# Lower parts of the first MLP's weights: subtracted on VectorE or on GpSimd

## The chip, the cores and the metric

The kernel runs on one core of a Trainium2 chip. The metric is the device time of one execution in microseconds (us). The engines are named as the profile names them: PE (TensorE matmul), PEld (its weight load), DVE (VectorE), ACT (ScalarE), POOL (GpSimd) and SP (the queue that issues all the DMAs here).

## The reference

An attention with pooled keys and values, then two MLPs, over 8 batches of 576 tokens (4608 rows of 512):

```
k_p, v_p = mean of k and v over each 8 neighbouring positions        # 72 keys per head
attn     = softmax(q k_p^T / sqrt(64)) v_p                           # 8 heads of 64
x        = attn as 4608 x 512
x        = (sigmoid(x @ w_gate) * (x @ w_val)) @ w_out               # d_ff 1536
out      = elu(x @ w_in2) @ w_out2                                   # d_ff 2048
```

`q`, `k`, `v` are float32. The five weight matrices are float64, and the kernel reads each as pairs of 32-bit integers.

## The kernel before

The matmuls take float32 operands in two parts, an upper one (`hi`, the value as `fp32r`) and a lower one (`lo`, the value less `hi`), and make three passes over them (`PASSES`). The 4608 tokens go in 12 blocks (`n`) of 384. In a block the first MLP loops over 12 columns of d_ff (`c`), 128 wide each: `emit_gate` for the gate (L493), `emit_sig` (L501), `emit_gate` for the value, `emit_g` (the product, L505, split into `hi` and `lo`), and for the column before, `emit_y` (L512). `emit_pv`, `emit_s`, `emit_t` and their like do the attention of the next block between these. The second MLP follows in six strips.

The weights of the first MLP must be narrowed from float64 to float32 and split before they are used. There are 36 jobs, three for each column (gate, value, out), and each is one 128x512 tile `nt`:

- `fetch_to`: a DMA brings the raw 64-bit words into a tile `rw` of the ring `raw` (4 buffers).
- `open_to`: ACT takes the magnitude of the high words into `nt` (L180; 3 buffers).
- `narrow_1`: two DVE instructions on `nt` (L102, L106).
- `narrow_2`: two DVE instructions that put in the sign and the low bits (L112, L116).
- `halves`, which calls `split`: ACT writes the upper part into `wg` or `wo` (L89), and POOL subtracts it from `nt` for the lower part (L90).

`convert` does one step of this pipe: it opens the job after the next, interleaves on DVE L112 of job i-1, L102 of job i, L116 of job i-1, L106 of job i, and then splits job i-1. Five calls of `convert` stand ahead of the first block, and block 0 calls it three times in each column. Below, A is the call between the two `emit_gate`, B the one behind the second, C the one behind `emit_g`. The jobs end in column 10 with `settle`, so that four splits lie ahead of block 0 and 32 in it. The order on every engine is the order of the code (`manual_schedule`), and each engine works through its own instructions in that order.

Besides these, POOL has in block 0 the lower part of `g` (L90, one per column), the normalization of the attention's weights `p` (L431), the lower part of the pooled values `vhl` (L368) and the placed values `vbd` (L376). The other callers of `split` for `pt` and `x` name DVE, and `emit_g` and the second MLP's `elu` leave it with POOL. The second MLP's weights are prepared in later blocks, where `lower` (L233) makes the same subtraction of 128x512 on DVE.

Of the kernel before, what the change touches and what calls it, by code (L numbers as in the profile page):

```python
# [9 lines left out]
F32 = mybir.dt.float32  # L10
# [14 lines left out]
def fused_kernel(  # L25
# [23 lines left out]
    nc = tc.nc  # L49
# [32 lines left out]
    def f32(ap):  # L82
        return ap.bitcast(F32)
# [4 lines left out]
    def split(dst_hi, dst_lo, src, eng=nc.gpsimd):  # L88
        nc.scalar.activation(out=dst_hi, in_=src, func=AF.Copy)  # L89
        eng.tensor_tensor(out=dst_lo, in0=src, in1=f32(dst_hi), op=ALU.subtract)  # L90
# [50 lines left out]
    def halves(dst):  # L141
        def done(t):
            hi, lo = dst()
            split(hi, lo, t.bitcast(F32))
        return done

    jobs = []
# [864 lines left out]
```

## Time and profile before

| | us |
|---|---|
| median of 3 runs | 1951.27 (1950.71 to 1951.61) |
| the profiled execution, its own time | 1944.64 |
| its span in the profile | 1942.9 |
| PE busy | 1842.2 (95%) |
| DVE busy | 915.6 (47%) |
| ACT busy | 794.0 (41%) |
| POOL busy | 509.3 (26%) |

The profiled execution took 1.74 us more than its span, and stands 6.6 us under the median of the runs. Times in the views count from the span's start. The busy share of an engine is an average over the whole program; the page also has it in 40 slices of 48.6 us, and the views of a stretch give it for a part of the program. In the rows, `out<-in` are the names of tiles, `xN` is the count, and what stands in brackets or behind the last bar is the time for which the engine sat idle before the instruction, and what ended it.

### The profile page before, as it was taken

How to read it: one execution, taken by the hardware profiler on the slowest of the kernel's cores; microseconds unless marked ns; L12 is line 12 of the kernel's file. 1: busy time of each engine (PE TensorE's matmuls, PEld its weight loads, DVE VectorE, ACT ScalarE, POOL GpSimd, SP SyncE). 2: the span in 40 equal slices, each digit the busy share in tenths (PEclk: the TensorE clock that was granted, in tenths of full speed). 3: DMA queues.
4: the chain of work that ended last, by engine and by line, in shares of the span. 5: the costliest groups of instructions: out<-in, count | busy, mean ns of one | idle time of the engine just before them, and what ended most of it. 6: DMA issues, size and time to landing. Idle time of an engine off the chain costs nothing.

```text
span 1942.9 us, 25840 instructions
## 1 busy us (share of the span) xinstructions
PE 1842.2 (95%) x9996; PEld 1735.3 (89%) x9996; DVE 915.6 (47%) x1531; ACT 794.0 (41%) x1499; POOL 509.3 (26%) x523
## 2 busy tenths in 40 slices
PE   4777999999989999899999999999999999999999
PEld 3666989989989999899999998989999998999988
DVE  7997445554545554533422223443444344443432
ACT  3544334333334343333333224444454444444443
POOL 4455212222213232113121112222222222222222
PEclk7889999999999999999999999999999999999999
DMA  7332224232223332320201244334343353343430
GB/s 216 109 124 87 79 82 126 97 96 79 80 90 117 111 102 93 95 73 23 63 3 28 77 146 188 127 125 168 114 179 118 125 190 125 132 163 135 163 114 33
DMA packets 112603, 213.49 MB, mean 110 GB/s; under 512 B 43616, under 2 KB 66656, under 8 KB 112480
## 3 DMA queue, kind: packets, MB, share of 16 engines
q1 hardware_dynamic: 112480, 211.84, 32.1%
q8 instruction: 78, 1.28, 0.3%
q14 instruction: 45, 0.37, 0.1%
HBM read 169.87 MB, written 41.94 MB: 109 GB/s over the span
## 4 chain that ended last, share of the span: by engine, by line
PE 61%; DVE 2%; DMA 1%; ACT 1%; issue 1%; SPq 0%; POOL 0%; DVEq 0%; ACTq 0%; POOLq 0%
PE oacc L893 20%; PE bank L847 18%; PE gv L493 13%; PE acc L512 7%; PE xv L473 1%; DVE ks L346 1%; PE atv L473 1%; PE ats L406 1%; DMA rkv<-in_k_dram 0%; DMA rw<-in_moe_w_out_dram 0%; PE att L446 0%; PE atq L396 0%; ACT L501 0%; DMA rkv<-in_v_dram 0%; DVE pt L90 0%
## 5 line engine op out<-in xcount | busy, mean ns | idle before, releaser
L493 PE MATMUL gv<-x,wg 128*128 128x384 f32 x3456 | 658.3, 344 | 20.2 <-DVE sg L505 18.5
L493 PEld LDWEIGHTS gv<-x,wg 128*128 128x128 f32 x3456 | 613.6, 193 | 25.7 <-ACT wo L89 11.9
L893 PE MATMUL oacc<-w2o,gc 128*128 128x512 f32 x1728 | 452.4, 393 | 2.8 <-ACT yl L536 2.5
L893 PEld LDWEIGHTS oacc<-w2o,gc 128*128 128x128 f32 x1728 | 319.1, 187 | 51.4 <-ACT yl L536 2.8
L847 PE MATMUL bank<-form,wr 128*128 128x384 f32 x1728 | 353.1, 339 | 1.5 <-DVE ea L860 1.4
L90 POOL TENSOR_TENSOR g<-sg,g 128x384 fp32r<-128x384 f32 x144 | 155.0, 1076 | 748.3 <-ACT g L89 748.3
L847 PEld LDWEIGHTS bank<-form,wr 128*128 128x128 f32 x1728 | 314.4, 188 | 25.2 <-DVE ea L860 1.7
L512 PE MATMUL acc<-g,wo 128*128 128x384 f32 x1728 | 327.0, 336 | 1.7 <-POOL g L90 1.7
L512 PEld LDWEIGHTS acc<-g,wo 128*128 128x128 f32 x1728 | 302.1, 188 | 5.0 <-POOL g L90 2.9
L505 DVE TENSOR_TENSOR sg<-sg,gv 128x384 f32<-128x384 f32 x144 | 79.3, 550 | 341.6 <-PE gv L493 341.1
L90 POOL TENSOR_TENSOR gc<-ea,gc 128x384 fp32r<-128x384 f32 x96 | 98.1, 1022 | 300.2 <-ACT gc L89 297.1
L90 POOL TENSOR_TENSOR gc<-eb,gc 128x384 fp32r<-128x384 f32 x96 | 97.9, 1019 | 261.3 <-ACT gc L89 240.8
L501 ACT ACTIVATE sg<-gv 128x384 f32<-128x384 f32 x144 | 70.7, 491 | 233.2 <-PE gv L493 232.9
L89 ACT ACTIVATE g<-sg 128x384 fp32r<-128x384 f32 x144 | 75.5, 524 | 178.0 <-DVE sg L505 177.9
L856 ACT ACTIVATE eb<-u 128x384 f32<-128x384 f32 x96 | 50.4, 525 | 129.5 <-DVE u L877 129.3
L860 DVE SCALAR_TENSOR_TENSOR eb<-eb,u 128x384 f32<-128x384 f32 x96 | 53.6, 558 | 99.6 <-ACT eb L857 99.6
L856 ACT ACTIVATE ea<-bank 128x384 f32<-128x384 f32 x48 | 23.6, 492 | 157.8 <-PE bank L847 157.8
L90 DVE TENSOR_TENSOR pt<-att,pt 128x512 fp32r<-128x512 f32 x72 | 34.7, 486 | 111.2 <-ACT pt L89 111.0
L860 DVE SCALAR_TENSOR_TENSOR ea<-ea,bank 128x384 f32<-128x384 f32 x48 | 26.6, 554 | 116.3 <-ACT ea L857 116.3
L871 DVE TENSOR_TENSOR u<-p,bank 128x384 f32<-128x384 f32 x48 | 26.6, 555 | 99.5 <-PE bank L847 97.3
L89 ACT ACTIVATE gc<-eb 128x384 fp32r<-128x384 f32 x96 | 50.4, 525 | 55.6 <-DVE eb L860 32.3
L89 ACT ACTIVATE gc<-ea 128x384 fp32r<-128x384 f32 x96 | 50.4, 526 | 55.3 <-DVE ea L860 55.3
(101 smaller groups left out, 1850.6 us busy)
## 6 DMA issues: line engine op xcount, KB each, us to landing
wr<-wd SPq DMA_DIRECT2D x96, 896.0 KB, 6.3
rw<-in_moe_w_out_dram SPq DMA_DIRECT2D x28, 512.0 KB, 3.6
r<-yd SPq DMA_DIRECT2D x24, 384.0 KB, 8.1
out_dram<-po SPq DMA_DIRECT2D x36, 256.0 KB, 2.0
yd<-yo SPq DMA_DIRECT2D x22, 384.0 KB, 3.1
rw<-in_moe_w_in_dram SPq DMA_DIRECT2D x16, 512.0 KB, 4.0
wd<-rw SPq DMA_DIRECT2D x16, 512.0 KB, 3.3
wod<-rw SPq DMA_DIRECT2D x16, 512.0 KB, 2.9
```

Of the source, the lines that this page charges most:

```text
L89: nc.scalar.activation(out=dst_hi, in_=src, func=AF.Copy)
L90: eng.tensor_tensor(out=dst_lo, in0=src, in1=f32(dst_hi), op=ALU.subtract)
L473: nc.tensor.matmul(d[j][:, o:o + w], lhsT=vb[:m, a_w].rearrange("p e d -> p (e d)"), rhs=p[:m, a_p, j + e, o:o + w], start=(e == 0 and a_w ...
L493: nc.tensor.matmul(d, lhsT=w[:, i, a_w, j], rhs=x[:, a_x, j], start=(j == 0 and a_w == 0 and a_x == 0), stop=(j == KD - 1 and a_w == 1),)
L501: nc.scalar.activation(out=sg, in_=gps, func=AF.Sigmoid)
L505: nc.vector.tensor_tensor(out=sg, in0=sg, in1=vps, op=ALU.mult)
L512: return lambda: nc.tensor.matmul(acc[m], lhsT=wo[c][:, a_w, m * P:(m + 1) * P], rhs=g[:, a_g], start=(c == 0 and a_w == 0 and a_g == 0), ...
L847: nc.tensor.matmul(bank[b ^ flip], lhsT=wp[q][a_w][:, w, j * P:(j + 1) * P], rhs=form_tile(s, a)[j][:, a_x], start=opens and n == 0, stop= ...
L856: nc.scalar.activation(out=e, in_=src, func=AF.Relu, scale=-1.0)
L860: nc.vector.scalar_tensor_tensor(out=e, in0=e, scalar=-1.0, in1=src, op0=ALU.add, op1=ALU.max)
L871: nc.vector.tensor_tensor(out=u2, in0=t_p1, in1=src, op=ALU.add)
L893: return lambda: nc.tensor.matmul(acc[t + i], lhsT=g[c][:, a_g, i * P:(i + 1) * P], rhs=wo2[2 * q + e][:, a_w], start=opens and p == 0, st ...
```

## The change

One argument: the function that splits the first MLP's weights gives `split` the engine DVE, where it left the default POOL.

```diff
     def halves(dst):
         def done(t):
             hi, lo = dst()
-            split(hi, lo, t.bitcast(F32))
+            split(hi, lo, t.bitcast(F32), nc.vector)
         return done
```

`split` itself stays:

```
    def split(dst_hi, dst_lo, src, eng=nc.gpsimd):
        nc.scalar.activation(out=dst_hi, in_=src, func=AF.Copy)
        eng.tensor_tensor(out=dst_lo, in0=src, in1=f32(dst_hi), op=ALU.subtract)
```

All 36 subtractions change the engine. PE, ACT and SP keep their instructions and their order. Two places show what moves.

DVE in column 3 of block 0, from the product (L505) over conversion C to the pooling of values; before:

```order
L505 TENSOR_TENSOR sg<-sg,gv 128x384
L112 SCALAR_TENSOR_TENSOR nt<-rw,nt 128x512
L102 TENSOR_SCALAR nt<-nt 128x512
L116 SCALAR_TENSOR_TENSOR nt<-rw,nt 128x512
L106 TENSOR_SCALAR nt<-nt 128x512
L365 TENSOR_REDUCE vs<-v_124 128x64
L367 CAST vhl<-vs 128x64
```

and with the change:

```order
L505 TENSOR_TENSOR sg<-sg,gv 128x384
L112 SCALAR_TENSOR_TENSOR nt<-rw,nt 128x512
L102 TENSOR_SCALAR nt<-nt 128x512
L116 SCALAR_TENSOR_TENSOR nt<-rw,nt 128x512
L106 TENSOR_SCALAR nt<-nt 128x512
L90 TENSOR_TENSOR wg_738<-nt,wg_738 128x512
L365 TENSOR_REDUCE vs<-v_124 128x64
L367 CAST vhl<-vs 128x64
```

The subtraction stands behind the four narrowing instructions, in front of all that DVE does next; it reads the upper part that ACT writes behind L116.

POOL over columns 3 and 4, from the lower part of one `g` to the next; before:

```order
L90 TENSOR_TENSOR g<-sg,g 128x384
L90 TENSOR_TENSOR wg_738<-nt,wg_738 128x512
L368 TENSOR_TENSOR vhl<-vs,vhl 128x64
L90 TENSOR_TENSOR wg_738<-nt,wg_738 128x512
L90 TENSOR_TENSOR wo_811<-nt,wo_811 128x512
L90 TENSOR_TENSOR g<-sg,g 128x384
```

and with the change:

```order
L90 TENSOR_TENSOR g<-sg,g 128x384
L368 TENSOR_TENSOR vhl<-vs,vhl 128x64
L90 TENSOR_TENSOR g<-sg,g 128x384
L368 TENSOR_TENSOR vhl<-vs,vhl 128x64
L431 TENSOR_TENSOR p<-p,sm 128x576
```

The three subtractions of the column are gone, and what is left stands in the same order.

## Rows read from the trace of the kernel before

**Rows 1.** The page, part 2: busy tenths in 40 slices.
```profile
PE   4777999999989999899999999999999999999999
...
DVE  7997445554545554533422223443444344443432
```
**Rows 2.** A 20 us stretch: busy us (count) of PE, PEld, DVE, ACT, POOL.
```profile
100.00:120.00 20.00, 13.98 (x79) 12.28 (x78) 19.79 (x30) 10.17 (x16) 10.47 (x9) 0.93 0.39 131
```
**Rows 3.** Groups of DVE, 49.6 to 181.9 us: busy us, mean ns, idle before.
```profile
L102 DVE TENSOR_SCALAR nt<-nt 128x512 f32<-128x512 f32 x31 | 31.1, 1002 | 0.2 <-ACT nt L180 0.2
L116 DVE SCALAR_TENSOR_TENSOR nt<-rw,nt 128x512 int32<-128x512 int32 x32 | 28.7, 897 | 0.0
L112 DVE SCALAR_TENSOR_TENSOR nt<-rw,nt 128x512 int32<-128x512 int32 x32 | 23.9, 747 | 0.3
L106 DVE TENSOR_SCALAR nt<-nt 128x512 int32<-128x512 int32 x31 | 16.9, 546 | 0.0
...
L429 DVE TENSOR_SCALAR sm<-sm 128x8 f32<-128x8 f32 x3 | 3.1, 1030 | 0.1
L367 DVE CAST vhl<-vs 128x64 fp32r<-128x64 f32 x4 | 2.9, 714 | 0.1
...
L90 DVE TENSOR_TENSOR pt<-att,pt 128x512 fp32r<-128x512 f32 x3 | 2.1, 692 | 6.2 <-ACT pt L89 6.2
...
L360 DVE COPY kbd<-atk 64x288 f32<-64x288 f32 x1 | 0.5, 460 | 0.7 <-ACT kbd L359 0.7
```
**Rows 4.** Groups of POOL, the same stretch.
```profile
L90 POOL TENSOR_TENSOR wg<-nt,wg 128x512 fp32r<-128x512 f32 x21 | 28.7, 1369 | 47.0 <-ACT wg L89 47.0
L90 POOL TENSOR_TENSOR wo<-nt,wo 128x512 fp32r<-128x512 f32 x10 | 16.8, 1684 | 18.2 <-ACT wo L89 18.2
L90 POOL TENSOR_TENSOR g<-sg,g 128x384 fp32r<-128x384 f32 x10 | 12.5, 1246 | 0.0
L431 POOL TENSOR_TENSOR p<-p,sm 128x576 f32<-128x576 f32 x3 | 4.3, 1419 | 1.2 <-DVE sm L430 1.2
```
**Rows 5.** DVE in order of time: start us, us, instruction.
```profile
23.46 0.17 DVE L429 TENSOR_SCALAR sm<-sm 128x8 f32<-128x8 f32 x1
...
32.36 0.20 DVE L367 CAST vhl<-vs 128x64 fp32r<-128x64 f32 x1
...
103.26 0.68 DVE L116 SCALAR_TENSOR_TENSOR nt<-rw,nt 128x512 int32<-128x512 int32 x1
103.86 0.41 DVE L106 TENSOR_SCALAR nt<-nt 128x512 int32<-128x512 int32 x1
104.30 0.69 DVE L112 SCALAR_TENSOR_TENSOR nt<-rw,nt 128x512 int32<-128x512 int32 x1
...
108.36 1.51 DVE L102 TENSOR_SCALAR nt<-nt 128x512 f32<-128x512 f32 x1
109.78 1.50 DVE L116 SCALAR_TENSOR_TENSOR nt<-rw,nt 128x512 int32<-128x512 int32 x1
```
**Rows 6.** POOL in order of time, at the last two of these and alone.
```profile
107.77 1.81 POOL L90 TENSOR_TENSOR wo<-nt,wo 128x512 fp32r<-128x512 f32 x1 [1.63 <-ACT wo L89]
109.54 1.20 POOL L90 TENSOR_TENSOR g<-sg,g 128x384 fp32r<-128x384 f32 x1
...
185.46 1.01 POOL L90 TENSOR_TENSOR g<-sg,g 128x384 fp32r<-128x384 f32 x1 [1.25 <-ACT g L89]
```
**Rows 7.** ACT in order of time: upper parts, and a late opening.
```profile
103.97 0.63 ACT L89 ACTIVATE wg<-nt 128x512 fp32r<-128x512 f32 x1 [1.04 <-DVE nt L116]
...
145.89 0.69 ACT L180 ACTIVATE nt<-rw 128x512 f32<-128x512 f32 x1 [3.01 <-DMA rw<-in_moe_w_val_dram]
146.47 0.63 ACT L89 ACTIVATE wo<-nt 128x512 fp32r<-128x512 f32 x1
```
**Rows 8.** SP in order of time: the issue of that raw tile.
```profile
142.29 0.37 SPq L121 DMA_DIRECT2D rw<-in_moe_w_val_dram  x1
```
**Rows 9.** Instructions on tile nt: ns min/median/max, first and last start.
```profile
L233 DVE TENSOR_TENSOR rw<-nt,rw x32: 673/683/1432, 212.9 to 844.5; 128x512 fp32r<-128x512 f32 x32
```
## The prediction, made before the changed kernel ran

> **What bounds the kernel now.** I read the page first. Over the whole program PE is busy 95% and DVE 47%, but the slices say that this is two programs in one: in the first four slices of 48.6 us DVE stands at 7, 9, 9 and 7 tenths and PE at 4, 7, 7 and 7, and only from the fifth or so on does PE fill its slices [rows 1]. All 36 splits lie in those first slices, so only that stage counts. A stretch of 20 us in its middle has DVE busy 19.79, PE 13.98, ACT 10.17, POOL 10.47 [rows 2]: DVE is the bound there, PE, ACT and POOL have room. The groups of DVE between 49.6 us (where block 0's conversions begin) and 181.9 us (where they end) show the same from the other side: hardly any idle in front of the narrowing instructions, 6.2 us in front of three `pt` and 0.7 us in front of one `kbd` [rows 3]. So the time of the stage is the time of DVE's own list, and the later program follows in one piece behind it.
>
> The second thing to see is that DVE's instructions do not all cost their own length. L106 takes 0.41 us and L112 or L116 0.68 us when nothing is beside them; L102 has the form of L106 and yet took 1.51, and the L116 behind it 1.50 [rows 5]. The POOL rows of those microseconds are a subtraction for `wo` from 107.77 and one for `g` from 109.54 [rows 6]: an instruction of DVE that starts beside one of POOL stretches by about 1 us, until POOL's has ended. In the groups L102 comes to a mean of 1.002 us instead of 0.41 [rows 3]. Part of DVE's list is therefore time lent to POOL, and the change takes away most of POOL's work in this stage: 31 subtractions and 45.5 us of its records, against 10 for `g` and 3 for `p` that stay [rows 4]. That is what makes the question open: DVE gets more work and less obstruction.
>
> **The change part by part.** It removes 36 subtractions from POOL and adds them to DVE; 32 of them lie in block 0 and 4 ahead of it. DMAs, ACT's and PE's instructions and the order of everything else stay.
>
> *The subtraction on DVE.* Its like is L233: same operation, shape and kinds, median 0.683 us [rows 9]. The next instruction on DVE starts about 0.08 us before the one in front has ended (L106 at 103.86 starts 0.08 before the end of L116 at 103.26 + 0.68 [rows 5]), so one takes 0.60 us of DVE's list.
>
> *The wait that it brings.* It needs ACT's upper part, and ACT starts that only behind L116. L116 ends at 103.94, ACT's `wg` starts at 103.97 and ends at 104.60 [rows 5, 7]; with 0.04 us more for the signal (the same step as from DVE to ACT) DVE could start the subtraction at 104.64. L106 would let the next instruction in at 103.86 + 0.41 - 0.08 = 104.19. So DVE stands still for 0.45 us and goes on at 105.24: 1.05 us in all. Where the next conversion follows directly, it starts at 104.30 today [rows 5], because it reads what L106 has just written, and then the cost is 0.94. I count 8 such places in block 0 by the order of the code and 24 others: 24 x 1.05 + 8 x 0.94 = **+32.7 us**. Bounds: 32 x 0.60 = 19.2 if every wait is covered, 33.6 if none is.
>
> *Where ACT is late.* Today nobody on DVE waits for the upper part, so ACT may be late; now DVE waits for it. Near the end the ring `raw` is short of one buffer for the next block's queries, and ACT stands for DMAs: a tile issued at 142.29 is opened at 145.89 and the upper part behind it starts at 146.47 [rows 7, 8], so the subtraction could start at 147.14, 4.9 us behind the end of the L116 that freed the buffer and so set the DMA off. Without that, the second of two conversions in a row would have its subtraction 0.70 + 0.60 + 1.62 + 0.70 = 3.6 us behind the first one's L116 (wait, subtraction, L112 to the end of L116, wait). That is 1.3 us late, and I expect it where A is followed by B in columns 7 and 9; column 8 has the normalization between. The very first conversion of block 0 is late by about as much, being behind a table load and the sigmoid on ACT, of which I take 1.0. Together **+3.6 us**; bounds 0 (DVE is slower, so the tiles are there in time) and 8 (all of the last three columns).
>
> *What POOL gives back.* Excess over the plain lengths, from the groups [rows 3] and the plain rows [rows 5]: L102 31 x (1.002 - 0.41) = 18.4, L116 32 x (0.897 - 0.68) = 6.9, L112 32 x (0.747 - 0.68) = 2.1, L106 31 x (0.546 - 0.41) = 4.2, L429 3 x (1.03 - 0.17) = 2.6, L367 4 x (0.714 - 0.20) = 2.1; together 36.3. What stays on POOL goes on costing: `g` takes 1.01 alone [rows 6] and still comes on in the middle of conversion C, `p` still stands in front of B's L102. I leave 1.0 for each of the 13 [rows 4], so that **-23.3 us** come back. Bounds: all 36.3 if POOL's remaining work falls into DVE's new waits; 22 if each costs 1.1, as L102 lost in rows 5.
>
> *Covers.* In front of `pt` and `kbd` DVE waits for ACT [rows 3]; the subtraction of C falls into that. In front of `kbd` that is 0.7. Of the three `pt`, two hang on the upper part of C through a table load and the sigmoid, and C's L116 ends about 1 us earlier with one obstruction less; the third hangs on the pooling of keys and gains nothing. **-2.7 us**; bounds 0 and 6.9.
>
> *Ahead of block 0.* Four subtractions, 4 x 1.05 = 4.2 at most, some of them in front of instructions that wait for PE or ACT anyway; I take half, **+2.0 us**.
>
> *POOL and PE.* POOL sat idle 47.0 and 18.2 us for upper parts in front of these subtractions [rows 4] so freeing POOL shortens nothing by itself; `g` and `vbd` come sooner, which is worth nothing while PE has a third of its time free [rows 2]. The lower parts are done sooner or as late as now, and PE needs them a column later. Costed at nothing; if PE were to wait for weights the cover is those 6 us in 20.
>
> Sum: 32.7 + 3.6 - 23.3 - 2.7 + 2.0 = **+12.3 us**. Against the profiled execution, 1944.64 + 12.3 = 1956.9; the median of the runs stands 6.6 higher, and it is what the forecast is for: 1951.27 + 12.3 = **1963.6 us**, 0.6% slower.
>
> **A rule of the Trainium skill.** The rows first: the subtraction takes POOL 1.37 or 1.68 us and DVE 0.68 [rows 4, 9], and POOL waits 65 us in front of its ones. The GPSIMD Engine Reference of the Trainium skill, section 4.1 Engine selection, says to put an elementwise operation on a tile on VectorE and not on GpSimd, which it gives as about twice as slow for two inputs. The trace agrees on the ratio; by the rule the change would be a gain, by the rows the engine that the work goes to is the full one. Its time is the second rival.
>
> **The rivals.**
> 1. *It costs more:* late upper parts in every conversion of the last three columns (9 instead of 2, but C is long enough not to be late, so some 4 us more) and waits nowhere covered (+2.7): about +19, 1970. For it: ACT's order is fixed and an upper part stands behind openings that wait for DMAs [rows 7]. Against: a slower DVE also issues fewer DMAs per time.
> 2. *Faster, the lent time outweighs:* the place is conversion C. If POOL's `g` (and `p` in B) gets its 1.01 us while DVE waits for ACT, and not in front of L116, all 36.3 come back; with no late upper part the sum is 32.7 + 0 - 36.3 - 2.7 + 2.0 = -4.3, 1947.0. Without late parts the sign turns where 32.0 of the 36.3 come back. For it: most of DVE's loss is POOL's doing. Against: DVE's wait is 0.45 long and comes behind L116, while `g` is ready for POOL about 1.2 us behind the start of the product (its length, ACT's upper part and two signals), which is during L102, and then holds up L116.
> 3. *No difference:* half of that, with `g` partly in waits, and 4 to 5 us of covers: -3 to +3, 1948 to 1954. It is the case too where PE and not DVE ended the stage, against which rows 2 speak.
>
> That the change does not move the work is excluded by the order: 36 rows leave POOL and 36 come to DVE.
>
> **How the numbers follow.** A measurement of this kernel can tell about 0.2%, 3.9 us, from no change. The forecast, +4 to +17, has 0.74; rival 1 has 0.12, rival 2 has 0.05, rival 3 has 0.09. So slower 0.86, same 0.09, faster 0.05. The bounds of the terms (late parts -3.6 to +4.4, given back 1.3 less to some 6 more, covers 2.7 less to 4.2 more, ahead of block 0 2 either way) do not all fall to one side; together I make them 8 below and 6 above: 1955.5 to 1969.5.
>
> **What would show it.** In the changed profile the mean of L102 should drop to about 0.5 us and that of L116 stay near 0.95 (or the two share one stretch of 1 us per column in another way); 36 subtractions of about 0.68 should stand on DVE with idle of about 0.45 in front of them, put down to ACT, some 15 to 20 us together; the product of column 10, at 181 us now, should come 10 to 13 us later, and everything behind it should keep its distance. POOL's busy time should fall by some 50 us. The prediction is wrong if the idle in front of the subtractions is near nothing, if L102 and L116 both stay plain in conversion C, or if PE is what the stage ends on.

## The result and the profile after

| | before | changed |
|---|---|---|
| median, us | 1951.07 (1950.71 to 1951.61, 4 runs) | 1965.58 (1962.88 to 1966.06, 4 runs) |
| profiled execution, its own time | 1944.64 | 1965.17 |
| its span | 1942.9 | 1963.4 |

The ratio is 1.0071, with a 95% interval of 1.0054 to 1.0089: the change made the kernel some 14 us slower. In a second comparison, told below, it was 1.0063 (1.0046 to 1.0081).

The page's slices, which answer to [rows 1]:

```profile
PE   3766999989989999989999999999999999999999
...
DVE  7887445555545454434332223434444344443432
```

DVE is less full in the first slices than it was, and the stage lasts longer all the same. The stretch of [rows 2], with the same columns, in the changed kernel:

```profile
100.00:120.00 20.00, 15.31 (x83) 14.60 (x84) 18.10 (x32) 9.41 (x16) 3.31 (x4) 0.91 0.49 154
```

DVE has gone from 19.79 to 18.10 busy although it has more to do, and POOL from 10.47 to 3.31: DVE's list now has holes. (The same 20 us do not hold quite the same instructions in the two kernels.) Which holes, the groups of DVE show (49 to 195 us, busy, mean ns, idle before; they answer to [rows 3]):

```profile
L116 DVE SCALAR_TENSOR_TENSOR nt<-rw,nt 128x512 int32<-128x512 int32 x32 | 30.0, 938 | 0.0
L112 DVE SCALAR_TENSOR_TENSOR nt<-rw,nt 128x512 int32<-128x512 int32 x32 | 21.7, 679 | 0.0
L102 DVE TENSOR_SCALAR nt<-nt 128x512 f32<-128x512 f32 x31 | 16.1, 520 | 0.0
L90 DVE TENSOR_TENSOR wg<-nt,wg 128x512 fp32r<-128x512 f32 x22 | 15.4, 699 | 8.9 <-ACT wg L89 8.9
L106 DVE TENSOR_SCALAR nt<-nt 128x512 int32<-128x512 int32 x31 | 13.3, 430 | 0.0
L90 DVE TENSOR_TENSOR wo<-nt,wo 128x512 fp32r<-128x512 f32 x11 | 7.6, 692 | 6.7 <-ACT wo L89 6.7
...
L90 DVE TENSOR_TENSOR pt<-att,pt 128x512 fp32r<-128x512 f32 x3 | 2.1, 692 | 4.5 <-ACT pt L89 4.5
...
L360 DVE COPY kbd<-atk 64x288 f32<-64x288 f32 x1 | 0.5, 462 | 0.0
```

L102 has fallen from 1002 ns to 520, L106 from 546 to 430, L112 is plain; L116 has risen from 897 to 938. The new subtractions take 0.69 to 0.70 us, and 15.6 us of idle stand in front of these 33, put down to ACT; one of the 33 stands ahead of block 0, and the 32 of block 0 have 15.3. One column of conversion C shows the whole pattern (DVE in order of time, column 3):

```profile
102.51 0.56 DVE L505 TENSOR_TENSOR sg<-sg,gv 128x384 f32<-128x384 f32 x1
102.99 0.68 DVE L112 SCALAR_TENSOR_TENSOR nt<-rw,nt 128x512 int32<-128x512 int32 x1
103.59 0.42 DVE L102 TENSOR_SCALAR nt<-nt 128x512 f32<-128x512 f32 x1
103.92 1.50 DVE L116 SCALAR_TENSOR_TENSOR nt<-rw,nt 128x512 int32<-128x512 int32 x1
105.35 0.41 DVE L106 TENSOR_SCALAR nt<-nt 128x512 int32<-128x512 int32 x1
106.12 0.69 DVE L90 TENSOR_TENSOR wg<-nt,wg 128x512 fp32r<-128x512 f32 x1 [0.36 <-ACT wg L89]
106.73 1.08 DVE L365 TENSOR_REDUCE vs<-v 128x64 f32<-128x512 f32 x1
```

and POOL in the same microseconds:

```profile
103.70 1.17 POOL L90 TENSOR_TENSOR g<-sg,g 128x384 fp32r<-128x384 f32 x1 [9.63 <-ACT g L89]
```

L102 is no longer held up; L116 is, by the one subtraction that POOL has kept in the column, and the new instruction starts 0.36 us behind the end of L106, when ACT's upper part is there. The L116 of conversion C takes 1.49 to 1.51 us in this way in all ten columns that have one (0 to 9).

How much the stage lost is read from the product of column 10, behind which the conversions are over. Before:

```profile
181.13 0.54 DVE L505 TENSOR_TENSOR sg<-sg,gv 128x384 f32<-128x384 f32 x1
```

changed:

```profile
193.23 0.55 DVE L505 TENSOR_TENSOR sg<-sg,gv 128x384 f32<-128x384 f32 x1
```

That is +12.1 us. Neither row has a wait in brackets: PE's `gv` lay ready, and DVE came to it late. At the last product of block 11 the difference of the two profiles is 20.5 us (1173.6 and 1194.1), and at the end again 20.5. The 8 us between were not forecast, and the first experiment is about them.

### The profile page after: what moved, and what is told of

Its sections match the earlier page's. It is cut to its first block, busy times and chain, and to the rows that moved or that the text cites. A ratio compares the mean times of both kernels' runs of the same rounds, so it can differ in the third digit from the quotient of the medians.

```text
span 1963.4 us, 25838 instructions
## 1 busy us (share of the span) xinstructions
PE 1849.4 (94%) x9996; PEld 1743.3 (89%) x9996; DVE 915.5 (47%) x1567; ACT 793.5 (40%) x1499; POOL 457.6 (23%) x487
## 4 chain that ended last, share of the span: by engine, by line
PE 60%; DVE 2%; DMA 2%; ACT 1%; issue 1%; SPq 0%; POOL 0%; ACTq 0%; DVEq 0%; POOLq 0%
PE oacc L893 20%; PE bank L847 18%; PE gv L493 13%; PE acc L512 6%; PE xv L473 1%; DMA rw<-in_moe_w_out_dram 1%; PE atv L473 1%; PE ats L406 1%; DVE ks L346 1%; DMA rkv<-in_k_dram 0%; PE att L446 0%; PE atq L396 0%; ACT L501 0%; DMA rkv<-in_v_dram 0%; DVE pt L90 0%
## 5 line engine op out<-in xcount | busy, mean ns | idle before, releaser
L493 PEld LDWEIGHTS gv<-x,wg 128*128 128x128 f32 x3456 | 618.8, 194 | 33.5 <-issue 29.7
L505 DVE TENSOR_TENSOR sg<-sg,gv 128x384 f32<-128x384 f32 x144 | 79.3, 551 | 343.8 <-PE gv L493 343.1
```

The source lines that it names most:

```text
L493: nc.tensor.matmul(d, lhsT=w[:, i, a_w, j], rhs=x[:, a_x, j], start=(j == 0 and a_w == 0 and a_x == 0), stop=(j == KD - 1 and a_w == 1),)
L505: nc.vector.tensor_tensor(out=sg, in0=sg, in1=vps, op=ALU.mult)
```

## The experiments

**The kernel before, once more**, for a second profile.

> The kernel before, unchanged, for a second profile. In the profiles the product of column 10 of block 0 stood at 181.1 us before and 193.2 with the change (+12.1), but the last product of block 11 at 1173.6 and 1194.1 (+20.5), and the median went up by 14.5. Theory: block 0 is the change's, the further 8 us (most of it between 630 and 700 us) vary from one execution to the next. Then the product of column 10 is at 181 +-0.3 again, and the span may be anywhere from 1942.9 to about 1950, with the difference in the stretch behind 600 us. Rival: the first profile was typical and the change costs the 8 us too; then the span is 1943 +-1.

The span was 1948.4 us (time 1950.27). The product of column 10 came at 181.5, just outside what was expected; the last product of block 11 at 1179.1 instead of 1173.6: 0.4 us of difference up to the product of column 10 and 5.1 more behind it, 3.5 of them in one place. There PE waits for the lower part of `pt`, the end of a chain over DVE and ACT that begins with a DMA of the keys. The start of the chain on DVE and its end on PE, in the first profile of before:

```profile
667.97 2.04 DVE L346 TENSOR_REDUCE ks<-rkv 128x64 f32<-128x512 f32 x2 [2.14 <-DMA rkv<-in_k_dram]
...
674.08 0.83 PE L356 MATMUL atk<-ident,ks 128*128 128x128 f32 x5 [1.94 <-DVE pt L90]
674.85 4.43 PE L493 MATMUL gv<-x,wg 128*128 128x384 f32 x24
```

and in the second:

```profile
669.43 2.04 DVE L346 TENSOR_REDUCE ks<-rkv 128x64 f32<-128x512 f32 x2 [2.42 <-DMA rkv<-in_k_dram]
...
675.54 1.38 PE L356 MATMUL atk<-ident,ks 128*128 128x128 f32 x5 [2.23 <-DVE pt L90]
676.86 6.88 PE L493 MATMUL gv<-x,wg 128*128 128x384 f32 x24
```

The wait for the DMA is 0.28 us longer here, that of PE 0.29. The same 24 matmuls took 4.43 us behind a wait of 1.94, and 6.88 behind one of 2.23. The stretches around them (busy us of PE, PEld, DVE, ACT, POOL, then the granted clock), first profile:

```profile
674.00:684.00 10.00, 9.92 (x59) 9.68 (x60) 5.83 (x10) 3.15 (x8) 2.66 (x3) 1.00 0.52 157
```

second profile:

```profile
675.00:685.00 10.00, 9.46 (x38) 9.04 (x39) 3.81 (x8) 3.10 (x7) 1.00 (x1) 0.66 0.36 105
```

TensorE's granted clock was 1.00 in the one and 0.66 as the mean of the other, so part of that stretch ran at 1.2 instead of 2.4 GHz. The first profile of the changed kernel has the same low stretch (0.66 from 690 to 700 us, behind a wait of 3.09), its second has not (1.00, behind 1.73). So the rival falls: two executions of one kernel differ there by 5.1 of the 8.3 us, and each of the two kernels has met the low stretch in one of its two profiles. That the longer wait brings the low clock is not shown: in a run told of below, a wait of 1.89, shorter than the 1.94 here, was followed by it too.

**The changed kernel, once more**, in one comparison with a run told of further below.

> The changed kernel again, for a second profile. Theory: block 0 repeats within 0.5 us (product of column 10 at 193.2), while the stretch between 600 and 850 us, in which ring buffers and DMAs set the pace, varies as it did between the two profiles of the kernel before (5 us). So the last product of block 11, at 1194.1 in the first profile, may be anywhere from 1186 to 1195. Rival: the change itself costs 8 us there; then it is at 1194 +-1.

The median was 1961.51 us against 1950.16, ratio 1.0063 (1.0046 to 1.0081). The product of column 10 came at 194.2, 1.0 later than expected; the product of column 0 is 1.0 later already (60.3 against 59.3), so that this arose at the start. The last of block 11 came at 1188.8, 5.3 us sooner than in the first profile. Against the second profile of before that is +9.7, against the first +15.1. From its first conversion to the product of column 10 block 0 takes 140.6 us, against 140.8 in the first profile; the stretch behind it does not repeat, and there the code of the two kernels is the same. The theory holds but for the start.

**The subtraction half a step later.** It stays on DVE, but its place is behind L112 and L102 of the next conversion.

```diff
-            split(hi, lo, t.bitcast(F32), nc.vector)
+            src = t.bitcast(F32)
+            nc.scalar.activation(out=hi, in_=src, func=AF.Copy)
+            lows1.append(lambda: nc.vector.tensor_tensor(out=lo, in0=src, in1=f32(hi), op=ALU.subtract))
...
-            for _ in range(2):
+            for half in range(2):
                 for t in turns:
                     next(t, None)
+                if half == 0:
+                    low1()
+                    open_to(i + 1 + peek)
```

`low1` issues what the list holds; `convert` opens only the next job ahead of the loop, since the magnitude after it needs the tile `nt` that the subtraction frees, and `settle` does the same.

> The subtractions stay on DVE, but each stands one half step later: behind L112 and L102 of the next conversion, when ACT has long written the upper part. Theory (the change costs 0.60 of DVE's list and 0.45 of waiting for ACT for each, and gives back some 23 of POOL's obstruction): the waits go, 32 x 0.45 = 14 and some of the late ones, so the product of column 10 comes at 177 to 180 us and the time is 13 to 17 us under the changed kernel, near the kernel before or up to 3 under it. Rival (the idle in front of the subtractions only stands where another wait would stand: DVE is held by ACT or by the DMAs of the raw tiles anyway): the product of column 10 stays at 190 to 194 us and the time within 3 us of the changed kernel.

1943.76 us against 1948.02 of the kernel before in the same comparison, ratio 0.9973 (0.9963 to 0.9983). The product of column 10:

```profile
176.91 0.55 DVE L522 TENSOR_TENSOR sg<-sg,gv 128x384 f32<-128x384 f32 x1
```

16.3 us sooner than in the changed kernel and 4.2 sooner than before: a tenth below the theory's 177, and the time is 4.3 under the kernel before where the theory had up to 3. The idle in front of the subtractions is 0.2 us in all, 15.1 less than in the changed kernel. So most of those waits were real time of DVE and not the shadow of another wait: the rival falls. Two smaller things lie beside them. 3.2 us came back as longer waits for ACT, in front of `pt` (7.3 against 5.5 with its small parts), `kbd` (0.7 against 0) and L102 (0.7 against 0); and `g` held DVE up in six columns instead of ten (below), worth some 3.3. About 1 us is left over. This version is faster than both kernels, by 0.27% under the kernel before.

**Nobody subtracts.** The kernel before, with zeros from ACT as the lower parts of the first MLP's weights; the third pass of the first MLP's matmuls then adds nothing.

```diff
-            split(hi, lo, t.bitcast(F32))
+            nc.scalar.activation(out=hi, in_=t.bitcast(F32), func=AF.Copy)
+            nc.scalar.activation(out=lo, in_=t.bitcast(F32), func=AF.Copy, scale=0.0)
```

> The kernel before with the 36 subtractions left out: ACT writes zeros as the lower parts of the first MLP's weights (ACT has some 10 us in 20 free), so neither POOL nor DVE has them. This is the price of POOL's work to DVE by itself. Theory: 23 us come back in block 0, since the rest of POOL's work (one g per column, three p) goes on obstructing; the product of column 10 at 156 to 162 us, the time 19 to 25 us under the kernel before, and L102 at a mean of about 0.5 us. Rival a (all of DVE's excess is due to these subtractions): 33 us or more. Rival b (the stretched lengths are not lost time, DVE would wait for ACT, PE or a DMA instead): under 8 us.

1926.88 us, ratio 0.9898 (0.9885 to 0.9911), 21 us less than before. The product of column 10:

```profile
158.02 0.55 DVE L506 TENSOR_TENSOR sg<-sg,gv 128x384 f32<-128x384 f32 x1
```

23.1 us sooner than before. The groups of L116 and L102 there:

```profile
L116 DVE SCALAR_TENSOR_TENSOR nt<-rw,nt 128x512 int32<-128x512 int32 x32 | 22.6, 707 | 0.0
...
L102 DVE TENSOR_SCALAR nt<-nt 128x512 f32<-128x512 f32 x31 | 16.6, 536 | 2.2 <-ACT nt L181 2.1
```

By the time, both rivals fall. But the exactness of the 23 is partly luck: reckoned as in the prediction, 29.7 us of the stretch came back and not 23.3, because the rest of POOL's work costs less here than forecast (L116 at 0.71 instead of 0.94: `g` meets other instructions once DVE runs ahead). Of the 29.7, 5.0 went into longer waits for ACT, which has more to write (`pt` 9.8 against 7.2, L102 2.1 against 0.2, `kbd` 1.2 against 0.7), and block 0 began 1.3 us later (51.0 against 49.6). From here to the changed kernel it is 193.23 - 158.02 = 35.2 us. That is only roughly the price of the subtractions on DVE with their waits, since the longer waits for ACT and the cheaper `g` are this run's own.

**The lower part of `g` on DVE too,** in block 0, in the same place as the subtraction of the run with the half step.

```diff
+        if first:
+            nc.scalar.activation(out=g[:, 0], in_=sg, func=AF.Copy)
+            lows1.append(lambda: nc.vector.tensor_tensor(out=g[:, 1], in0=sg, in1=f32(g[:, 0]), op=ALU.subtract))
+        else:
+            split(g[:, 0], g[:, 1], sg)
```

> As the run before the last (subtractions on DVE, half a step later), and in block 0 the lower part of g too is subtracted by DVE in that place, so that POOL keeps only p, vhl and vbd there. Theory: one g costs DVE 0.82 us today by holding up L116 in conversion C and would cost 0.47 of its list, so 10 to 11 times 0.35, 3 to 4 us less than with the subtractions alone in that place, and L116 at its plain 0.68. Rival (POOL's g fell into time that DVE has free): 5 us more.

A miss. 1947.06 us, ratio 0.9991 (0.9981 to 1.0000), and the product of column 10 at 177.0, the same as without this step. Even that is so only because block 0 began 1.1 us earlier (51.3 against 52.4): from there to the product it took 125.6 us against 124.5. L116 was nearly plain at 0.695 us as expected; but in the run without this step `g` had not cost what I took. Two rows of POOL there, columns 4 and 5:

```profile
107.21 2.71 POOL L90 TENSOR_TENSOR g<-sg,g 128x384 fp32r<-128x384 f32 x1 [5.52 <-ACT g L89]
...
119.79 1.17 POOL L90 TENSOR_TENSOR g<-sg,g 128x384 fp32r<-128x384 f32 x1 [2.92 <-ACT g L89]
```

and DVE in column 4 and at two instructions of column 5:

```profile
107.09 0.42 DVE L102 TENSOR_SCALAR nt<-nt 128x512 f32<-128x512 f32 x1
107.43 0.68 DVE L146 TENSOR_TENSOR wo<-nt,wo 128x512 fp32r<-128x512 f32 x1
108.03 0.68 DVE L116 SCALAR_TENSOR_TENSOR nt<-rw,nt 128x512 int32<-128x512 int32 x1
108.63 0.42 DVE L106 TENSOR_SCALAR nt<-nt 128x512 int32<-128x512 int32 x1
108.97 1.06 DVE L382 TENSOR_REDUCE vs<-v 128x64 f32<-128x512 f32 x1
...
119.67 0.41 DVE L102 TENSOR_SCALAR nt<-nt 128x512 f32<-128x512 f32 x1
120.01 1.50 DVE L146 TENSOR_TENSOR wo<-nt,wo 128x512 fp32r<-128x512 f32 x1
```

In column 5 POOL got in behind L102, and the subtraction on DVE was held up (1.50 instead of 0.68). In column 4 POOL's instruction starts at the same place, 0.12 us behind the start of L102, but DVE went on through three instructions without a gap, and POOL took 2.71 us instead of the 1.01 that it takes alone: it waited some 1.7. So it went in columns 0, 2, 4 and 6; in 1, 3, 5 and 8 POOL got in; in 7 and 9 it came a step later and held up L116. So `g` cost 6 x 0.82 = 4.9 us and not 8 or 9, and its 10 subtractions ahead of the product of column 10 cost 10 x 0.47 = 4.7 on DVE. The two cancel, and the waits in front of `pt` grew by 1.3 us (8.6 against 7.3). That the whole run was 3.3 us slower than without the step arose behind block 0. In the profiles 2 of the 3.2 us that arose there lie at the place of the first experiment:

```profile
672.04 0.93 PE L373 MATMUL atk<-ident,ks 128*128 128x128 f32 x5 [1.89 <-DVE pt L90]
672.89 5.86 PE L510 MATMUL gv<-x,wg 128*128 128x384 f32 x24
```

The granted clock was 0.83 from 672 to 682 us here, and 1.00 in the same place (670 to 680) without the step. Whether the step makes that more frequent, so that the medians of 12 runs each differ, stays open.

**The query's load later.** The changed kernel, with one line of `plan` altered:

```diff
-                early[3 * i + 1].append(("ldq", t + 1))
+                early[3 * i + 1 if n > 1 else C1 - 2].append(("ldq", t + 1))
```

> The changed kernel, with the one query tile that block 0 loads for block 1 (it takes one of the four buffers of the raw tiles from column 7 on) loaded in column 10. In the changed profile three subtractions of block 0 wait 1.4 to 1.6 us for ACT where the others wait 0.36: one in column 0 and the ones of B in columns 7 and 9. Theory: the last two are late because the ring of raw tiles is short of one, so ACT stands for a DMA; they go back to 0.36 and the product of column 10 comes 2.2 to 2.6 us earlier, at 190.6 to 191.1. Rival (the DMAs themselves or ACT's order make them late): it stays at 193.2. The whole time should show 2.5 us less at most, which the spread of the runs may hide.

The subtraction of B in column 7, in the changed kernel:

```profile
153.67 0.69 DVE L90 TENSOR_TENSOR wo<-nt,wo 128x512 fp32r<-128x512 f32 x1 [1.60 <-ACT wo L89]
```

ACT in front of it:

```profile
152.46 0.66 ACT L180 ACTIVATE nt<-rw 128x512 f32<-128x512 f32 x1 [2.99 <-DMA rw<-in_moe_w_val_dram]
```

and the same subtraction with the later load:

```profile
152.16 0.69 DVE L90 TENSOR_TENSOR wo<-nt,wo 128x512 fp32r<-128x512 f32 x1 [0.36 <-ACT wo L89]
```

From the product of column 6 to that of column 10 it took 48.95 us, against 51.58 in the changed kernel: 2.6 less, at the upper end of the theory. The product of column 10 came at 190.3, 0.3 beyond what was expected, and these 0.3 arose before column 6. The median, 1960.88 against 1961.51 of the changed kernel in the same comparison, does not tell the two apart.

## Why the prediction was right

Step by step, with the numbers of the changed profile:

- *That the stage is DVE's.* Right. None of the products of columns 0 to 10 waits for PE, before or after, and the end of the stage moved when stretch was taken off DVE's list (23.1 us of the 29.7) or waits (16.3, with 15.1 of waits gone).
- *The subtraction and its wait, +32.7, and late upper parts, +3.6.* Right. (The places where a conversion follows directly are 9 and not 8, which is 0.1 us.) The view of DVE's waits puts 15.3 us of block 0 down to ACT's upper parts of these weights; the view counts from the end of L106, 0.08 us behind the point from which the estimate counts, so 15.3 + 32 x 0.08 = 17.9, against 32 x 0.45 + 3.6 = 18.0. The late ones stood where they were expected: column 0 (1.44) and B of columns 7 and 9 (1.60 and 1.51), which is 1.1 to 1.2 over the usual 0.36; the forecast said 1.0 and 1.3.
- *What POOL gives back, -23.3.* Right for this kernel. By the same reckoning the excess left is L102 31 x 0.11 = 3.4, L116 32 x 0.258 = 8.3, L106 0.6, and some 0.4 on the subtractions: 12.7 where 13.0 were left. It was `g` on L116 (ten of 0.82) and `p` on L102 (three of about 1), as said. The price of 1.0 for each is the step that does not carry over: for `g` it was 0.82 here, and in the run with the half step nothing in four of ten columns.
- *Covers, -2.7.* The idle in front of `pt` fell from 6.2 to 4.5 and that in front of `kbd` from 0.7 to 0: 2.4.
- *Ahead of block 0, +2.0.* The first conversion of block 0 starts at 52.4 instead of 49.6: +2.7 (in the second profiles at 53.5 instead of 49.9: +3.6). The 2.0 was half of a bound and no reckoning; that it came close is luck.
- *Sum.* +12.3 forecast, +12.1 at the product of column 10. That is 9.4 in block 0, where the terms give 10.3, and 2.7 ahead of it, where 2.0 stood, so that two small misses make the sum better than its parts. The medians differ by 14.5 in the first comparison and 11.4 in the second.
- *What was wrong:* that "everything behind it should keep its distance". Behind block 0 two executions of one and the same kernel differ by 5 us, so that a difference of two profiles (20.5) says less than either the column-10 product or the medians.
- *The rivals.* The faster one needed `g` to fall into DVE's new waits; it fell on L116 in ten columns. No difference was excluded by the interval. The costlier one needed late upper parts in all of the last columns; there were two, and the one in column 0.
- *The rule on engines.* By the Trainium skill's GPSIMD Engine Reference, section 4.1 Engine selection, the subtraction belongs on VectorE. The ratio in its favour is here (0.69 against 1.37 to 1.68 us), and still the kernel got slower, because VectorE was the full engine of the stage. The run with the half step shows the rest: the same engine, a place where the subtraction need not wait, and 0.27% faster than before.

## What to carry to other kernels

Before work moves to the engine that bounds a stage, add up two things beside its own length: what the new instruction waits for at its place in that engine's list (here 0.45 us beside 0.60 of work), and what the engine that gives it up took from the others by running beside them (here 23 of the 36 us that DVE's instructions were stretched). In a list that is worked through in order, an instruction that needs another engine's answer is better placed behind other work than right behind its cause: here half a step later was worth 16 us. And a profile's total is compared at the end of the stage that was changed, with a second profile of the same kernel to show what the rest does by itself.

## What was not expected of the hardware

- POOL and DVE beside each other, in the run with the half step: at the same place in DVE's list (0.11 to 0.12 us behind the start of L102) POOL's subtraction for `g` got in at once in four columns (DVE held up by 0.82 us) and waited some 1.7 us in four others, through three DVE instructions in a row. What decides between the two is not shown.
- At one place behind block 0, a wait of PE of 2.23 us was followed by a granted clock of 0.66 over the next 10 us, one of 1.94 by 1.00, and one of 1.89 in another run by 0.83; the same 24 matmuls took 6.88, 4.43 and 5.86 us. The length of the wait alone does not tell which.
